# Linear attention with a highway layer on one core: batch 5's queries turned by DMA, one more x block added on GpSimd, and a new list of steps

## The chip, the core and the metric

The kernel runs on one core of a Trainium2 chip. The core has five engines with an instruction queue each: TensorE (PE: matrix products, and turning blocks by a product with the identity), VectorE (DVE), ScalarE (ACT), GpSimd (POOL), and SyncE (SP), which here only issues DMAs. Every queue runs in order: an instruction that waits holds up all that stand behind it. Sixteen DMA engines move data between HBM and the core's SBUF; TensorE writes into PSUM. The metric is the time of one execution on the device in microseconds (us); lower is better.

## The reference, cut to what matters

Eight batches, eight heads, 576 tokens, 64 channels per head; all inputs and the output are float32.

```python
# attention: q, k, v are (8, 8, 576, 64)
q_s = exp(q - max(q, -1));  q_s = q_s / sum(q_s, -1)      # softmax over channels
k_s = exp(k - max(k, 2));   k_s = k_s / sum(k_s, 2)       # softmax over tokens
kv  = einsum('bhsd,bhse->bhde', k_s, v)                   # 64 x 64 per head
x   = einsum('bhsd,bhde->bhse', q_s, kv)                  # then (4608 tokens, 512)
# highway layer: w_h, w_t are (512, 512)
H = maximum(x @ w_h, 0)
T = 1 / (1 + exp(-(x @ w_t + b_t)))
out = T * H + (1 - T) * x
```

## The kernel before

The kernel never subtracts the maxima. It works in float16 between the float32 loads and stores. The layer's output is written as x + (1 + tanh) * max(ph, -x/2), where ph comes from halved weights from which the identity was taken (`less_one`, `cast_weight` with 0.5), and tanh from half of the gate.

All 64 head rows of a batch are handled as four blocks of 128 partitions (two heads each). A token index is p * 9 + n, so a batch has nine groups n of 64 tokens. Groups 0 to 7 of two batches share one tile `xT` (a pair: batches 0 and 1 are pair 0, and so on). The ninth groups of all batches are collected in `x9` and handled at the end as two more "batches", 8 and 9, of half the width.

Per batch b the steps are:

- `load`: q, k and v by one or two DMAs each, on SP. Each of the three has three buffers; the two weight matrices borrow a buffer of q and of k.
- `exp_half` on ScalarE (two for q, two for k), `cast_v` on GpSimd or `cast_v_head` on GpSimd or ScalarE.
- `q_sums` or `q_sums_tree`, then `q_recip` on VectorE, and `q_scale_v` (VectorE, batch 0) or `q_scale_p` (GpSimd) to scale the queries.
- turning the scaled queries so that channels lie on partitions: `q_trans` (TensorE, 18 matmuls a batch in three groups, into PSUM) and `q_copy` (VectorE, one per group), or `q_turn`: a DMA transpose from SBUF to SBUF, in two pieces. Which batches use `q_turn` is in the tuple `turned`.
- `kv_half` twice on TensorE (72 small matmuls in all) and `kv_norm` on VectorE.
- `x_pair` twice on TensorE gives x; `x_copy` on ScalarE or VectorE takes it out of PSUM. For batches from 3 on the ninth group comes with it and `x9_done` copies it; before, `x_left` does.
- for each of four output blocks ob: `gate` (four matmuls with w_t) and `tanh` on ScalarE; `carry` (four matmuls with w_h) and `diff` on VectorE; `blend` on VectorE.
- the rest, "+ x", in one of two ways: `add_x` on GpSimd, for the blocks named by `added`; for the others `out_tile` adds x inside PSUM, by an extra matmul of x with the identity.
- `out_tile` turns a group of a pair back to rows of tokens: four matmuls, and one more for each block that `added` doesn't name. `out_copy` takes it to SBUF, and after each fourth group a 1 MB DMA stores it. `tile9`, `tile9_copy` and `last9` do the same for the ninth groups.

The order of all this is written out by hand, or by a program that the source doesn't contain, as one list, `order`. The kernel runs through it and issues each step as it comes, so the list fixes the order on each engine's queue, and the DMA queue of SP as well. Loads of batches 0 and 1 and of the weights stand ahead of the list, in the order q 0, k 0, v 0, bias, w_t, q 1, w_h, k 1, v 1. `warm_up` and `warm_mid` are matmuls whose result nobody reads.

Of the kernel before, what the change touches and what calls it, by code (L numbers as in the profile page):

```python
# [18 lines left out]
def kernel(  # L19
# [81 lines left out]
    def load_weight(n, w, tag, parts=1):  # L101
        t = ld.tile([P, 4, N9, 64], FP32, tag=tag, name=f"w32{n}")
        w32[n] = t.rearrange("p c n d -> p (c n d)")[:, 0:2048].rearrange(
            "p (k n) -> p k n", k=4
        )
        view = w.rearrange("(k p) n -> p k n", p=P)
        step = 4 // parts
        for k_ in range(0, 4, step):
            nc.sync.dma_start(w32[n][:, k_ : k_ + step], view[:, k_ : k_ + step])
# [13 lines left out]
    for w in "qkv":  # L123
        load(0, w, 2)
    nc.sync.dma_start(brow, moe_b_t.rearrange("(k p) -> k p", p=P))
    load_weight("t", moe_w_t, "q32")
    load(1, "q")
    load_weight("h", moe_w_h, "k32", 4)
    load(1, "k")
    load(1, "v", 2)  # L130
# [28 lines left out]
    def bank(home, name, dt=FP32):  # L159
        if home == "q2":  # L160
            return two_banks(name, dt)[:, 0]
        ps = {"ht": ps_ht, "q1": ps_1, "nat": ps_nat}[home]
        return ps.tile([P, 512 if dt is FP32 else 1024], dt, tag=home, name=name)

    def warm_mid(n):
        t = bank("q1", "warm_mid")
        for _ in range(n):
            mm(t, ident, wide, True, True)
# [112 lines left out]
    turned = (6, 7)  # L281
# [140 lines left out]
    added = lambda g: ((0, 1), (0, 1), (0, 1), (0, 1, 2, 3))[g]  # L422
# [73 lines left out]
    def last9():  # L496
# [10 lines left out]
        for f in (  # L507
            add_x, blend, carry, cast_v, cast_v_head, cast_weight, diff, exp_half, gate,
            gate_bias, kv_half, kv_norm, last9, less_one, load, out_copy, out_tile, q_copy,
            q_recip, q_scale_p, q_scale_v, q_sums, q_sums_tree, q_trans, q_turn, tanh,  # L510
            tile9, tile9_copy, warm_mid, warm_up, x9_done, x_copy, x_left, x_left_copy,
            x_pair,
        )
    }
    order = [
        ("warm_up", 24), ("exp_half", 0, "q", 1), ("warm_up", 6), ("q_sums", 0, 1),
        ("exp_half", 0, "q", 0), ("q_sums", 0, 0), ("load", 2, "q"), ("cast_v", 0, 0),
        ("q_recip", 0), ("q_scale_v", 0, 4, 9), ("warm_up", 1), ("cast_v", 0, 1),
        ("q_trans", 0, 1, "q2"), ("cast_weight", "t", 1, "P"), ("q_scale_v", 0, 0, 4),
        ("q_copy", 0, 1), ("warm_up", 4), ("exp_half", 0, "k", 1), ("q_trans", 0, 2, "nat"),  # L520
        ("q_trans", 0, 0), ("q_copy", 0, 0), ("kv_half", 0, 1), ("exp_half", 0, "k", 0),
        ("kv_half", 0, 0), ("cast_weight", "t", 3, "P"), ("kv_norm", 0),
        ("cast_weight", "t", 2, "V"), ("q_copy", 0, 2), ("x_pair", 0, 0, False),
        ("x_pair", 0, 1, False, ("ht", "ht")), ("x_copy", 0, 0, "AA"), ("less_one", 0),
        ("gate_bias",), ("x_copy", 0, 1, "AV"), ("warm_up", 2), ("exp_half", 1, "q", 0),
        ("cast_weight", "t", 0, "V"), ("q_sums_tree", 1, 0), ("exp_half", 1, "q", 1),
        ("warm_mid", 5), ("cast_weight", "h", 0, "A", 0.5), ("less_one", 2),
        ("less_one", 3), ("gate", 0, 0), ("q_sums_tree", 1, 1), ("q_recip", 1),
        ("cast_weight", "h", 3, "A", 0.5), ("cast_weight", "h", 2, "A", 0.5),
        ("less_one", 1), ("x_left", 0), ("q_scale_p", 1, 0, 4), ("gate", 0, 2, "q2"),  # L530
        ("x_left_copy", 0), ("load", 2, "v", 2), ("load", 2, "k"),
        ("cast_weight", "h", 1, "A", 0.5), ("q_scale_p", 1, 4, 8), ("warm_up", 2),
        ("tanh", 0, 0), ("tanh", 0, 2), ("cast_v_head", 1, 2, "P"), ("warm_up", 2),
        ("exp_half", 1, "k", 0), ("gate", 0, 1), ("tanh", 0, 1), ("carry", 0, 0),
        ("carry", 0, 1), ("diff", 0, 0), ("q_trans", 1, 0), ("diff", 0, 1),
        ("cast_v_head", 1, 1, "P"), ("carry", 0, 2), ("q_copy", 1, 0),
        ("cast_v_head", 1, 0, "A"), ("carry", 0, 3), ("load", 3, "k"), ("q_trans", 1, 1),
        ("diff", 0, 2), ("load", 3, "q"), ("blend", 0, 2), ("exp_half", 1, "k", 1),
        ("cast_v_head", 1, 3, "A"), ("q_copy", 1, 1), ("kv_half", 1, 0), ("kv_half", 1, 1),
        ("exp_half", 2, "q", 0), ("blend", 0, 0), ("exp_half", 2, "q", 1), ("kv_norm", 1),  # L540
        ("x_pair", 1, 0, False, ("ht", "ht")), ("blend", 0, 1), ("x_copy", 1, 0, "AV"),
        ("cast_v_head", 2, 0, "P"), ("x_pair", 1, 1, False, ("ht", "q2")),
        ("q_sums_tree", 2, 0), ("x_copy", 1, 1, "AV"), ("q_scale_p", 1, 8, 9),
        ("q_trans", 1, 2), ("gate", 0, 3, "nat"), ("cast_v_head", 2, 3, "A"),
        ("q_copy", 1, 2), ("gate", 1, 0), ("q_sums_tree", 2, 1), ("tanh", 0, 3),
        ("q_recip", 2), ("carry", 1, 0), ("diff", 0, 3), ("add_x", 0, 1),
        ("cast_v_head", 2, 1, "A"), ("load", 3, "v"), ("x_left", 1),
        ("exp_half", 2, "k", 1), ("diff", 1, 0), ("blend", 0, 3), ("carry", 1, 1),
        ("diff", 1, 1), ("tanh", 1, 0), ("q_scale_p", 2, 0, 4), ("cast_v_head", 2, 2, "P"),
        ("gate", 1, 1), ("exp_half", 2, "k", 0), ("tanh", 1, 1), ("x_left_copy", 1),  # L550
        ("gate", 1, 2), ("load", 4, "q"), ("q_trans", 2, 0, "q1"), ("kv_half", 2, 0),
        ("blend", 1, 0), ("q_copy", 2, 0), ("kv_norm", 2, 0, 1), ("blend", 1, 1),
        ("q_scale_p", 2, 4, 8), ("q_scale_p", 2, 8, 9), ("carry", 1, 2), ("add_x", 0, 0),
        ("add_x", 1, 1), ("q_trans", 2, 1, "q1"), ("diff", 1, 2), ("load", 4, "v"),
        ("tanh", 1, 2), ("q_copy", 2, 1), ("exp_half", 3, "k", 0), ("exp_half", 3, "q", 0),
        ("carry", 1, 3), ("load", 4, "k"), ("cast_v", 3, 0), ("kv_half", 2, 1),
        ("x_pair", 2, 0, False, ("nat", "q1")), ("gate", 1, 3), ("blend", 1, 2),
        ("x_copy", 2, 0, "AA"), ("kv_norm", 2, 1, 2),
        ("x_pair", 2, 1, False, ("nat", "q1")), ("exp_half", 3, "q", 1), ("q_sums", 3, 0),
        ("q_trans", 2, 2, "q2"), ("x_copy", 2, 1, "AV"), ("cast_v", 3, 1), ("load", 5, "q"),  # L560
        ("carry", 2, 0), ("q_sums", 3, 1), ("q_copy", 2, 2), ("exp_half", 3, "k", 1),
        ("gate", 2, 0), ("x_left", 2), ("diff", 2, 0), ("tanh", 1, 3), ("tanh", 2, 0),
        ("carry", 2, 1), ("exp_half", 4, "q", 0), ("q_recip", 3), ("diff", 1, 3),
        ("gate", 2, 2), ("blend", 2, 0), ("gate", 2, 1), ("blend", 1, 3), ("add_x", 1, 0),
        ("load", 6, "q"), ("x_left_copy", 2), ("out_tile", 0, 1), ("q_scale_p", 3, 0, 4),
        ("tanh", 2, 2), ("diff", 2, 1), ("tanh", 2, 1), ("blend", 2, 1),
        ("q_trans", 3, 0, "q1"), ("kv_half", 3, 0), ("q_scale_p", 3, 4, 9),
        ("kv_half", 3, 1), ("out_copy", 0, 1, "A"), ("out_tile", 0, 0), ("q_copy", 3, 0),
        ("kv_norm", 3), ("out_copy", 0, 0, "A"), ("cast_v", 4, 1), ("q_trans", 3, 1, "q1"),
        ("cast_v", 4, 0), ("q_trans", 3, 2, "q2"), ("carry", 2, 2), ("q_copy", 3, 1),  # L570
        ("q_copy", 3, 2), ("x_pair", 3, 0, True), ("q_sums", 4, 0), ("add_x", 2, 1),
        ("exp_half", 4, "q", 1), ("x_copy", 3, 0, "A"), ("out_tile", 0, 2), ("diff", 2, 2),
        ("gate", 2, 3), ("load", 5, "k"), ("out_copy", 0, 2, "A"), ("x_pair", 3, 1, True),
        ("carry", 2, 3), ("q_sums", 4, 1), ("q_recip", 4), ("load", 5, "v"),
        ("blend", 2, 2), ("x_copy", 3, 1, "A"), ("out_tile", 0, 3), ("carry", 3, 0),
        ("add_x", 2, 0), ("out_copy", 0, 3, "A"), ("x9_done", 3), ("load", 6, "v"),
        ("diff", 3, 0), ("tanh", 2, 3), ("out_tile", 0, 4), ("exp_half", 5, "q", 0),
        ("gate", 3, 0), ("q_scale_p", 4, 0, 4), ("q_scale_p", 4, 4, 9), ("gate", 3, 1),
        ("tanh", 3, 0), ("diff", 2, 3), ("blend", 3, 0), ("out_copy", 0, 4, "A"),
        ("q_trans", 4, 0, "q1"), ("carry", 3, 1), ("exp_half", 4, "k", 1),  # L580
        ("out_tile", 0, 5), ("q_copy", 4, 0), ("diff", 3, 1), ("q_trans", 4, 1, "q1"),
        ("tanh", 3, 1), ("gate", 3, 2), ("q_copy", 4, 1), ("kv_half", 4, 1),
# [105 lines left out]
```

## Time and profile before

| what | value |
|---|---|
| median of 5 runs | 129.31 us (128.53 to 129.94) |
| the profiled execution | 128.05 us |
| its span in the profile | 125.9 us |
| read from HBM, written | 30.41 MB, 9.44 MB |
| share of the DMA queue, over 16 engines' span | 85.1% |
| granted clock of TensorE, mean | 0.986 |

The profile counts from the first instruction. Rows of the timeline give a start, a length (of several instructions where "xN" stands), the engine, the line, the operation, "out<-in" by the program's names, and in brackets how long the engine had been idle before and what ended that. Tiles are named as in the program: `eq` and `ek` are the exponentials of q and k, `pq` and `qsT` the turned queries in PSUM and in SBUF, `qsD` those turned by DMA, `psk` and `kvn` the product of k and v, `px` and `xT` x, `pt` and `ph` the gate and the carry, `dd` and `g` the results of `diff` and `blend`, `nat` an output tile, `o` its copy.

The times that matter for what follows: the first gate starts at 17.80 us, the eight matmuls of `x_pair` of batch 1 at 29.95, `kv_half` of batch 3 at 52.02. Two pieces of batch 6's `q_turn` are issued from 81.88 on, of batch 7's from 92.50 on. The last matmul starts at 121.90, the last store is issued at 122.55.

### The profile page before, as it was taken

To read this page: it belongs to the slowest core of one execution; us is meant where nothing else is said; L and a number is where in the kernel's file an instruction comes from. 1 tells how busy PE (TensorE), PEld (TensorE's weight loads), DVE (VectorE), ACT (ScalarE), POOL (GpSimd) and SP (SyncE) were. 2 spreads that over 40 slices of the span, in tenths; PEclk is the share of its full clock that TensorE was granted. 3 is DMA by queue.
4 is the path that set the end of the run, shared out by engine and by line. 5 is a ranking of instruction groups with operands and counts; after the bars stand their busy time and mean duration, and the time that the engine had idled before them with its cause. 6 is when DMAs were issued, how large, how long until landed. Compare 5 with 4: busy or idle time off the path is not lost.

```text
span 125.9 us, 3361 instructions
## 1 busy us (share of the span) xinstructions
PE 111.5 (89%) x1375; PEld 62.0 (49%) x1375; DVE 96.4 (77%) x179; ACT 93.2 (74%) x130; POOL 75.6 (60%) x71
## 2 busy tenths in 40 slices
PE   4998599585599989999999998999999999999940
PEld 1344443252235534746554475555556455589820
DVE  1079749299958999899799988879966549799960
ACT  4156085995877698688998988999998895576640
POOL 2005623960779577996972895699797224855500
PEclk9999999999869999999999999999999999999999
DMA  3999999999999999999999999969427716008994
GB/s 103 386 402 404 391 403 408 411 413 410 405 411 411 407 406 412 413 402 411 420 409 409 405 412 412 424 154 278 164 50 165 303 81 260 5 42 359 421 366 150
DMA packets 20583, 41.24 MB, mean 327 GB/s; under 512 B 5460, under 2 KB 5976, under 8 KB 19544
## 3 DMA queue, kind: packets, MB, share of 16 engines
q1 hardware_dynamic: 20568, 41.03, 85.1%
q8 instruction: 10, 0.16, 0.5%
q14 instruction: 5, 0.04, 0.1%
HBM read 30.41 MB, written 9.44 MB: 316 GB/s over the span
## 4 chain that ended last, share of the span: by engine, by line
PE 51%; DMA 24%; DVE 12%; ACT 5%; issue 2%; POOL 2%; DVEq 1%; POOLq 1%; SPq 0%
PE ph L64 19%; PE pt L64 18%; DMA v<-in_v_dram 10%; DMA w32h<-in_moe_w_h_dram 10%; PE nat L64 7%; DMA q<-in_q_dram 4%; DVE g L417 3%; PE pq L69 3%; PE px L64 2%; DVE r L228 2%; DVE dd L409 2%; ACT pt L396 1%; DVE qsT L278 1%; PE psk L64 1%; DVE kvn L217 1%
## 5 line engine op out<-in xcount | busy, mean ns | idle before, releaser
L258 POOL TENSOR_TENSOR eq<-eq,r 128x1024 f16<-128x1024 f16 (+2 forms) x16 | 29.8, 1879 | 9.6 <-DVE r L246 8.7
L64 PE MATMUL ph<-xT,w16h 128*128 128x512 f16 x128 | 33.4, 387 | 2.3 <-ACT w16h L114 1.6
L64 PE MATMUL pt<-xT,w16t 128*128 128x512 f16 x128 | 32.8, 388 | 0.0
L409 DVE SCALAR_TENSOR_TENSOR dd<-xT,ph 128x512 f16<-128x512 f16 x32 | 21.5, 678 | 10.4 <-PE ph L64 9.2
L396 ACT ACTIVATE pt<-pt,bt 128x512 f32<-128x512 f32 (+1 forms) x40 | 24.5, 622 | 6.7 <-PE pt L64 6.5
L428 POOL TENSOR_TENSOR g<-g,xT 128x512 f16<-128x512 f16 x19 | 21.7, 1154 | 9.1 <-DVE g L417 8.3
L417 DVE SCALAR_TENSOR_TENSOR g<-pt,dd 128x512 f16<-128x512 f32 (+1 forms) x40 | 24.7, 627 | 2.3 <-ACT pt L396 1.1
L178 ACT ACTIVATE eq<-q 128x1152 f16<-128x1152 f32 x16 | 18.4, 1165 | 5.5 <-DMA q<-in_q_dram 5.5
L64 PEld LDWEIGHTS <-w16h 128*128 128x128 f16 x160 | 14.4, 99 | 14.7 <-issue 2.3
L64 PEld LDWEIGHTS <-w16t 128*128 128x128 f16 x160 | 14.9, 99 | 13.2 <-issue 1.9
L189 POOL CAST v<-v 128x1152 f16<-128x1152 f32 x12 | 14.3, 1209 | 11.5 <-DMA v<-in_v_dram 11.4
L178 ACT ACTIVATE ek<-k 128x1152 f16<-128x1152 f32 x16 | 18.7, 1172 | 2.1 <-DMA k<-in_k_dram 2.1
L228 DVE TENSOR_REDUCE r<-eq 128x18 f32<-128x1152 f16 x12 | 16.0, 1344 | 5.3 <-ACT eq L178 5.3
L468 ACT COPY o<-nat 128x512 f32<-128x512 f32 x28 | 16.6, 592 | 4.5 <-PE nat L64 4.0
L64 PE MATMUL nat<-ident,g 128*128 128x128 f16 x142 | 16.2, 219 | 0.1
L64 PEld LDWEIGHTS <-g 128*128 128x128 f16 x144 | 12.4, 98 | 6.5 <-DVE g L417 1.1
L64 PE MATMUL warm<-wide,ident 128*128 128x512 f16 x41 | 11.8, 444 | 1.8 <-DVE wide L149 1.8
L361 ACT CAST xT<-px 128x1024 f16<-128x1024 f32 x10 | 10.2, 1018 | 1.8 <-PE px L64 1.5
L69 PE MATMUL pq<-ident,eq 128*128 128x128 f16 x108 | 9.0, 219 | 2.4 <-POOL eq L258 1.8
L278 DVE COPY qsT<-pq 128x1024 f16<-128x1024 f16 (+1 forms) x18 | 9.9, 552 | 1.5 <-PE pq L69 1.1
L69 PEld LDWEIGHTS <-eq 128*128 128x128 f16 x108 | 6.9, 98 | 5.7 <-POOL eq L258 2.1
L64 PEld LDWEIGHTS <-ident 128*128 128x128 f16 x46 | 4.9, 109 | 8.2 <-issue 3.4
(53 smaller groups left out, 105.7 us busy)
## 6 DMA issues: line engine op xcount, KB each, us to landing
out_dram<-o SPq DMA_DIRECT2D x8, 1024.0 KB, 4.6
q<-in_q_dram SPq DMA_DIRECT2D x7, 1152.0 KB, 13.6
k<-in_k_dram SPq DMA_DIRECT2D x7, 1152.0 KB, 13.4
v<-in_v_dram SPq DMA_DIRECT2D x5, 1152.0 KB, 14.5
v<-in_v_dram SPq DMA_DIRECT2D x6, 576.0 KB, 12.1
q<-in_q_dram SPq DMA_DIRECT2D x2, 576.0 KB, 4.1
k<-in_k_dram SPq DMA_DIRECT2D x2, 576.0 KB, 6.6
w32t<-in_moe_w_t_dram SPq DMA_DIRECT2D x1, 1024.0 KB, 10.6
```

The source lines that it names most:

```text
L64: mm = lambda o, l, r, st, sp: nc.tensor.matmul(o, l, r, start=st, stop=sp, skip_group_check=True)
L69: nc.tensor.matmul(o, i, ident, is_transpose=True, start=True, stop=True, skip_group_check=True,)
L178: nc.scalar.activation(dst[b][:, :, 2 * a : 2 * a + 2, :], in32[which][b][:, 2 * a : 2 * a + 2].rearrange("p c n d -> p n c d"), AF.Exp,)
L189: nc.gpsimd.tensor_copy(o, i)
L228: nc.vector.reduce_sum(qsum[b][:, :, h], eq[b][:, :, h, :], axis=AX.X)
L258: nc.gpsimd.tensor_mul(e, e, r.broadcast_to(list(e.shape)))
L278: nc.vector.tensor_copy(qsT[b][:, :, n0:n1, :], turned_q.pop((b, g)))
L396: nc.scalar.activation(ps, ps, AF.Tanh, bias=bt2[:, ob : ob + 1], scale=0.5)
L409: nc.vector.scalar_tensor_tensor(dd, xv(ob), -0.5, ps, op0=ALU.mult, op1=ALU.max)
L417: nc.vector.scalar_tensor_tensor(gv(ob), th, 1.0, dd, op0=ALU.add, op1=ALU.mult)
L428: eng.tensor_add(gv(ob), gv(ob), xv(ob))
L468: copy(rows_of_four((g, n // 4))[:, n % 4, :], nat.pop((g, n)))
```

## The change

Four things change:

1. `turned` becomes (5, 6, 7): batch 5's queries are turned by two DMA transposes; its three `q_trans` and three `q_copy` leave the list. They are cut at group 5, not 4.
2. `added` names block 2 too for pairs 1 and 2: four more `add_x` on GpSimd (batches 2 to 5), and 16 matmuls less in `out_tile`.
3. The loads ahead of the list move into it, and the whole list is remade. Q of batch 1 is now loaded first and Q of batch 2 ahead of V and K of batch 1.
4. `warm_mid` takes a name and a bank; three calls stand in the list, one after the last step.

```diff
-    for w in "qkv":
-        load(0, w, 2)
-    nc.sync.dma_start(brow, moe_b_t.rearrange("(k p) -> k p", p=P))
-    load_weight("t", moe_w_t, "q32")
-    load(1, "q")
-    load_weight("h", moe_w_h, "k32", 4)
-    load(1, "k")
-    load(1, "v", 2)
+    def load_bias():
+        nc.sync.dma_start(brow, moe_b_t.rearrange("(k p) -> k p", p=P))
...
-    def warm_mid(n):
-        t = bank("q1", "warm_mid")
+    def warm_mid(n, i=None, home="q1"):
+        t = bank(home, "warm_mid" if i is None else f"warm_{i}")
...
-    turned = (6, 7)
+    turned = (5, 6, 7)
...
-    added = lambda g: ((0, 1), (0, 1), (0, 1), (0, 1, 2, 3))[g]
+    added = lambda g: ((0, 1), (0, 1, 2), (0, 1, 2), (0, 1, 2, 3))[g]
...
     order = [
+        ("load", 1, "q"), ("load", 0, "q", 2), ("load", 0, "k", 2), ("exp_half", 1, "q", 0),
+        ("q_sums_tree", 1, 0), ("load_bias",), ("exp_half", 0, "q", 0), ("load", 0, "v", 2),
+        ("warm_up", 24), ("warm_mid", 5), ("exp_half", 1, "q", 1), ("cast_v", 0, 0),
...
+        ("q_scale_v", 0, 4, 9), ("warm_mid", 2, 0), ("load_weight", "t", "q32"),
+        ("q_scale_p", 1, 0, 4), ("q_scale_v", 0, 0, 4), ("load_weight", "h", "k32", 4),
...
+        ("cast_weight", "h", 1, "A", 0.5), ("load", 2, "q"), ("less_one", 2),
+        ("q_trans", 0, 1, "q2"), ("warm_up", 1), ("load", 1, "v", 2), ("q_copy", 0, 0),
+        ("q_copy", 0, 1), ("x_pair", 0, 0, False), ("x_copy", 0, 0, "AA"), ("less_one", 3),
+        ("load", 1, "k"), ("gate_bias",), ("q_trans", 1, 0), ("less_one", 0),
...
+        ("load", 2, "k"), ("exp_half", 2, "q", 0), ("load", 2, "v", 2), ("q_copy", 1, 0),
+        ("warm_up", 2), ("q_scale_p", 1, 4, 8), ("x_copy", 0, 1, "AV"),
+        ("cast_weight", "t", 3, "P"), ("load", 3, "q"), ("warm_up", 2),
+        ("exp_half", 2, "q", 1), ("cast_weight", "t", 2, "V"), ("q_copy", 0, 2),
+        ("x_left", 0), ("x_left_copy", 0), ("q_sums_tree", 2, 0), ("warm_up", 2),
+        ("cast_weight", "t", 1, "P"), ("cast_weight", "h", 0, "A", 0.5), ("gate", 0, 0),
+        ("cast_weight", "h", 3, "A", 0.5), ("tanh", 0, 0), ("q_sums_tree", 2, 1),
...
+        ("x_pair", 4, 1, True), ("exp_half", 6, "q", 1), ("add_x", 2, 2), ("x9_done", 4),
+        ("q_turn", 5, 5, 9), ("x_copy", 4, 1, "A"), ("cast_v", 6, 0), ("cast_v", 5, 1),
+        ("gate", 3, 3), ("out_tile", 0, 6), ("exp_half", 5, "k", 0), ("diff", 3, 0),
+        ("blend", 3, 1), ("diff", 3, 3), ("gate", 3, 0), ("q_sums", 6, 1), ("add_x", 2, 0),
+        ("out_copy", 0, 6, "A"), ("tanh", 3, 0), ("q_turn", 5, 0, 5), ("carry", 4, 0),
+        ("carry", 4, 2), ("kv_half", 5, 1), ("diff", 4, 0), ("blend", 3, 0),
+        ("kv_half", 5, 0), ("load", 7, "v"), ("tanh", 3, 3), ("kv_norm", 5),
+        ("out_tile", 0, 7), ("add_x", 2, 1), ("exp_half", 6, "q", 0), ("gate", 4, 0),
+        ("tanh", 4, 0), ("gate", 4, 2), ("add_x", 3, 0), ("add_x", 3, 2), ("diff", 4, 2),
+        ("add_x", 3, 1), ("q_sums", 6, 0), ("x_pair", 5, 0, True), ("blend", 3, 3),
...
+        ("tanh", 9, 3), ("blend", 9, 2), ("diff", 9, 3), ("tile9", 3, 3), ("tile9", 2, 3),
+        ("tile9_copy", 2, 3, "A"), ("tile9_copy", 3, 3, "V"), ("blend", 9, 3), ("last9",),
+        ("warm_mid", 2, 3),
     ]
```

On SP's queue the loads now stand as q 1, q 0, k 0, bias, v 0, w_t, w_h, q 2, v 1, k 1, k 2, v 2, q 3, q 4, v 3, k 3, q 5, v 4, k 4, k 5, v 5, q 6, v 6, q 7, then the first output block, the two pieces of batch 5's `q_turn`, v 7, k 6, the second output block, batch 6's `q_turn`, k 7, the third output block, batch 7's `q_turn`. Before, after v 5 came the first output block, then v 6, k 6, k 7, q 7, v 7, the second output block and batch 6's `q_turn`; q 6 stood ahead of k 5.

## The prediction

> **What bounds the kernel now.** I read the page's busy shares and 40 slices, then the chain of waits, then TensorE's timeline, then the DMA rows.
>
> ```profile
> PE 111.5 (89%) x1375; PEld 62.0 (49%) x1375; DVE 96.4 (77%) x179; ACT 93.2 (74%) x130; POOL 75.6 (60%) x71
> PE   4998599585599989999999998999999999999940
> DMA  3999999999999999999999999969427716008994
> ```
>
> Two limits follow each other. The DMA digits stand at 9 up to slice 26, about 82 us: inputs arrive as fast as they can. TensorE (PE) is ragged for its first ten or so slices and solid from slice 14 to the end. So early on, the order of loads decides; later, the number of matmuls.
>
> ```profile
> 18.42 12.86 DMA v<-in_v_dram
> 31.42 0.67 POOL v L197
> 32.09 0.64 POOL eq L258
> 32.77 0.28 PE pq L69 x2
> ```
>
> The chain around 32 us (start, length): TensorE waits for batch 1's last queries, scaled by GpSimd (POOL), which stood behind a cast of batch 2's V, which waited for its load. TensorE's windows (PE busy, granted clock) show the second price:
>
> ```profile
> 31.00:32.00 1.00, 0.00 (x0) 1.00 1.05 415
> 32.00:33.00 1.00, 0.23 (x3) 1.00 1.05 408
> 34.00:35.00 1.00, 1.00 (x4) 0.50 1.03 408
> 36.00:37.00 1.00, 1.00 (x4) 0.50 1.03 406
> 38.00:39.00 1.00, 1.00 (x7) 1.00 1.05 415
> ```
>
> After the hole the clock is halved for some 3.4 us: 1.7 us of matmul time lost.
>
> ```profile
> 44.76 2.24 POOL L189 CAST v<-v 128x1152 f16<-128x1152 f32 x2 [1.12 <-DMA v<-in_v_dram]
> 64.82 2.24 POOL L189 CAST v<-v 128x1152 f16<-128x1152 f32 x2 [0.90 <-DMA v<-in_v_dram]
> 78.17 0.22 PE L64 MATMUL px_l<-qsT,kvn 64*64 64x64 f16 x2 [0.32 <-DVE kvn L217]
> ```
>
> The timeline's first two rows give landings of V of batches 3 and 5. Seven loads lie between: (64.82 - 44.76) / 7 = 2.87 us a load of 1.18 MB. The third is the start of x_pair 5, my measuring point.
>
> **A count of TensorE's work.** From starts in the timeline, a gate or carry of four 512-wide matmuls takes 0.86 us (batches 8 and 9: 0.44), a turning matmul 0.057 (0.45 for 8), kv_half 0.42, x_pair 0.34 to 0.40, an out_tile of six 0.34. Along the list this makes 92.5 us before. Time minus work ahead is the debt: kv_half 3 has 26.9 us ahead of it and starts at 52.0, debt 25.1; x_pair 5 has 51.3 and starts at 78.2, debt 26.9; the last matmul ends at about 122.1, debt 29.5.
>
> **Part 1, matmuls removed.** 18 turning matmuls of batch 5 (18 x 0.057 = 1.0 us) and, with block 2 of x no longer added in PSUM for pairs 1 and 2, 2 x 8 = 16 of 0.056 (0.9 us). Work falls to 90.6 us; it lies where TensorE is solid, so 1.9 us is the gain if debts stay. VectorE loses three q_copy (2 x 0.687 + 0.283 = 1.7 us), worth nothing by itself while TensorE is the bound.
>
> **Part 2, added on GpSimd.** Four add_x of 1.154 us (row L428), 4.6 us. What waits behind: add_x(2,2) stands before the casts that kv_half 5 needs. GpSimd takes V 5 at 61.9 (below), scales batch 5 to 67.5, then add_x 1.1 and two casts of 1.1 each: ready at 70.8. kv_half 5 has 45.0 us ahead and with a debt of 27 asks at 72. add_x(3,2) precedes scaling of batch 6, which waits for VectorE's reciprocal anyway (a 2.69 us wait in row 79.95 before); those of pair 2 come after the scaling of batch 7. I cost them at nothing, with about 1 us of cover; without it, up to 1.1 us for each of the first two.
>
> **Part 3, the DMA turns of batch 5.** Two instructions on SP. All loads before them keep the stream full, and V 5 is now one load earlier in it (q 6 follows): 64.8 - 2.9 = 61.9. q 6, v 6, q 7 land at 64.8, 67.7, 70.6, the first output block (1.05 MB) at 73.1. The turns are issued when GpSimd has scaled: the reciprocal comes at 63.3 by VectorE's queue, 2.3 + 1.9 us of scaling, so 65.6 and 67.5. Both queue behind that output. Their length:
>
> ```profile
> 92.40:95.70 3.30, 3.30 (x26) 1.88 (x25) 2.13 (x4) 3.00 (x5) 3.30 (x3) 1.00 0.41 79
> qsD<-eq SPq DMA_TRANSPOSE x4, 3.3
> ```
>
> The window (last two columns: DMA share, GB/s) holds one turn of 8 of a batch's 18 blocks: 0.41 x 3.3 = 1.35 us of all engines, so 18/8 x 1.35 = 3.0 us a batch. [...] v 7 and k 6 stand behind the turn on SP, k 7 behind that of batch 6: they land near 79, 82 and 90.5, and kv_half 6 and 7 ask near 85.5 and 95.5; hidden. The two warm matmuls put at the very end (0.43 us) lie beside the last store (issued at 122.55, 2 us to the end).
>
> **Part 4, the list.** q 1 is loaded first, so batch 0 and w_t arrive one load (2.9 us) later: V 0 ends at 15.1 instead of 12.2, w_t at 17.7 instead of 14.9. q 2 moves ahead of v 1 and k 1; V and K of batch 1 are complete at 29.9 instead of 27.0. K and V of batch 2 end at 36.1 as before. The first gate ran at 17.8; now its x copy stands on ScalarE behind exp of q 2 (lands 24.2), so it runs near 25.7. w_h arrives at 21.3 either way and its last cast follows at 27.9, so carries start there. Then kv_half 1 waits for exp of k 1 (29.9, two exps and a cast: 32.7), x_pair 1 ends at 35.2, kv_half 2 waits for V 2 (36.1) and two GpSimd casts: 37.5. carry(1,1) ends at 39.3 with 14.4 us of work behind it: debt 24.9, against 23.7 before at 40.2. Between the warm-up's end near 11.8 us (31 matmuls end at 10.9 before, 35 now) and kv_half 0 near 14.9 TensorE idles 3 us, and is thin after; add 0.7 us for a halved clock: debt 25.6, 1.9 behind.
>
> [...] I take 0.7 and leave 0 to 1.7 for the range.
>
> From 40 to 48 us VectorE runs without pause in both lists (sums of batch 3 sit between the diffs); kv_half 3 comes at 24.0 + 26.8 = 50.8, debt 26.8, 1.7 behind. Up to x_pair 5 before lost 1.8 us more; I give the new list 1.5 (fewer copies): it has 47.9 us ahead, 47.9 + 28.3 = 76.2, just as the turn lands.
>
> **Sum.** From x_pair 5: 90.6 - 47.9 = 42.7 us of work, plus the 2.6 us before lost from there to its end, minus 0.3, as VectorE has less left when gate(9,0) runs (5.6 against 8.5 us of durations). 76.2 + 42.7 + 2.3 = 121.2 against 122.1: -0.9. The span becomes 125.0, the profiled run's 128.05 becomes 127.15. It lies 1.26 below the median of 129.31 (runs 128.53 to 129.94), so 128.4.
>
> **Rivals.**
> *Forecast, 0.42:* as summed, own range 127.2 to 129.6. Half of it is over 1% faster or nearly so: I give 0.2 to faster, 0.22 to within.
> *Everything saved is kept, 0.20:* the early debt is made up where VectorE has fewer copies, and turns land at 74.6; end 74.9 + 42.7 + 1.9 = 119.5, 126.7 us. For: TensorE need not be solid before 50 us. Against: VectorE has no pause there.
> *The turn of batch 5 lands late, 0.24; slower:* every middle load takes 12 to 14 us from issue to landing ("q<-in_q_dram" 13.6). If the stream is still that deep at 67.5, the second half lands at 67.5 + 13 = 80.5, 4.3 late: 132.7; half as deep, 131. TensorE runs in order, so all behind x_pair 5 moves with it. It decides from x_pair 5 after 78.4 on (0.9 + 1.3 past 76.2). For: GpSimd scales batch 5 only behind a cast that waits for V 5. Against: SP must first wait for the output block's copy near 62, which drains the stream.
> *Four full engines, 0.14:* from 50 to 76 us VectorE, ScalarE and GpSimd each have about 23 us of work for TensorE's 24 (rows' durations summed along the list, less what successive ones overlap: 0.60 us apart where the row says 0.68), GpSimd some 2 us more than before. 1.5 us more of waits: 129.9.
>
> **Numbers.** About 1% is what a measurement of this kernel can tell from no change. Faster: 0.2 + 0.2 = 0.40. Within: 0.22 + 0.06 of the full engines = 0.28. Slower: 0.24 + 0.08 = 0.32. The range 126.2 to 131.6 leaves out the ends of second and third case.
>
> **What would show it.** TensorE near 90 us without warm-ups; first gate at 25 to 26 us; kv_half 3 at 50 to 52; x_pair 5 at 76 waiting for qsD at most 1 us; no hole from 80 to the tail. A first gate before 22 or an x_pair 5 after 78.4 proves me wrong, as does a GpSimd add as the releaser of output tiles.

## The result, and the profile after

The changed kernel took 127.76 us in the median of 44 runs, the kernel before 129.17 us in 79. The ratio is 0.9949, 95% interval [0.9924, 0.9974]: a small gain. It is not the quotient of the two medians (0.989), because it compares only the fast runs of each kernel, those within 1.5% of its fastest. The prediction was 128.4 us. Run once more beside the last experiments, the same changed kernel came to 0.9865 [0.9816, 0.9914]. The two intervals do not meet, so ratios from different groups of runs can't be compared more finely than about 1%. Below, small differences are therefore read in the traces, from one event to another.

The profiled execution took 128.16 us, its span is 126.2. That of before had 128.05 and 125.9. Taken alone the two would say "no change"; why they mislead comes out of the clock row, in 9 below. From the page of the changed kernel, the busy shares and three rows of the 40 slices:

```profile
PE 111.1 (88%) x1345; PEld 61.7 (49%) x1345; DVE 95.7 (76%) x176; ACT 92.0 (73%) x130; POOL 79.5 (63%) x75
PE   4997314899998999999999999999997999999960
PEclk9999965569999999999999999999999999999999
DMA  3999999999999999999999999989997530089994
```

Before, TensorE was ragged to slice 13; now the digits are thin in slices 4 to 6 (12 to 22 us) and nearly solid behind that, with one 7 near 97 us. The clock row has a half-speed stretch where TensorE is thin. From the timeline (TensorE) and the DMA rows of the changed kernel, the two that answer to x_pair 5 and to the turns:

```profile
76.83 0.22 PE L64 MATMUL px_l<-qsD,kvn 64*64 64x64 f16 x2
```

```profile
qsD<-eq SPq DMA_TRANSPOSE x6, 5.3
```

x_pair 5 starts at 76.83 us with no wait in brackets: batch 5's turned queries were there. Its two pieces were issued at 67.92 and 69.78 and landed at 73.64 and 74.75.

The head, in windows of 6 us (stretch, its length, busy time of PE, PEld, DVE, ACT and POOL with the number of instructions, granted clock, DMA share, GB/s):

```profile
12.00:18.00 6.00, 1.49 (x74) 0.94 (x73) 5.15 (x9) 1.77 (x2) 3.00 (x3) 0.91 1.05 410
18.00:24.00 6.00, 2.86 (x21) 1.99 (x21) 4.59 (x7) 0.63 (x1) 6.00 (x7) 0.50 1.05 407
24.00:30.00 6.00, 6.00 (x44) 3.00 (x41) 3.80 (x11) 5.34 (x8) 1.42 (x3) 0.74 1.04 411
```

TensorE works 1.49 of the first 6 us while VectorE works 5.15. In the next window the clock is 0.50: it was halved from 16.9 to 27.2 us. The first gate starts at 29.01 us; 25.7 was predicted. TensorE's two long waits of that stretch:

```profile
14.60 0.48 PE L64 MATMUL psk<-v,ek 64*64 64x65 f16 x36 [2.68 <-POOL v L185]
20.79 1.89 PE L69 MATMUL pq<-ident,eq 128*128 128x128 f16 x16 [4.28 <-DVE eq L250]
```

The second is for VectorE's scaled queries. VectorE's and GpSimd's rows show what came before them:

```profile
14.89 1.25 DVE L236 TENSOR_TENSOR t<-t 128x288 f16<-128x288 f16 x1
17.96 1.88 DVE L248 CAST r<-r 128x32 f16<-128x32 f32 x1
```

```profile
14.83 1.15 POOL L185 CAST v<-v 128x1152 f16<-128x1152 f32 x1 [0.28 <-DMA v<-in_v_dram]
17.30 2.50 POOL L254 TENSOR_TENSOR eq<-eq,r 128x1024 f16<-128x1024 f16 x1 [1.32 <-DVE r L248]
```

Two small instructions of VectorE end just behind an instruction of GpSimd that they lie over: 16.14 behind 15.98, and 19.84 behind 19.80. The scaling on GpSimd took 2.50 us; the eight others of its size (the next one at 21.75) took 1.90.

A hole that before did not have, from ScalarE's and TensorE's timelines:

```profile
94.46 2.22 ACT L174 ACTIVATE ek<-k 128x1152 f16<-128x1152 f32 x2 [2.10 <-DMA k<-in_k_dram]
```

```profile
97.20 0.33 PE L64 MATMUL nat<-ident,g 128*128 128x128 f16 x3 [0.73 <-ACT o L464]
```

ScalarE waits 2.10 us for K of batch 7. The copy of an output tile stands behind it on ScalarE, and TensorE needs the bank which that copy frees: 0.73 us lost. K 7 was issued at 85.97 and landed at 94.38.

### The profile page after: what moved, and what is told of

Same layout as the page of the kernel before. It is cut to its first block, busy times and chain, and to the rows that moved or that the text cites. A ratio compares the mean times of both kernels' runs of the same rounds, so it can differ in the third digit from the quotient of the medians.

```text
span 126.2 us, 3307 instructions
## 1 busy us (share of the span) xinstructions
PE 111.1 (88%) x1345; PEld 61.7 (49%) x1345; DVE 95.7 (76%) x176; ACT 92.0 (73%) x130; POOL 79.5 (63%) x75
## 4 chain that ended last, share of the span: by engine, by line
PE 69%; DVE 11%; DMA 6%; ACT 4%; POOL 3%; issue 2%; SPq 1%; DVEq 1%; ACTq 0%
PE pt L64 23%; PE ph L64 21%; PE nat L64 8%; DMA k<-in_k_dram 6%; PE pq L69 5%; PE psk L64 4%; PE px L64 4%; PE warm L64 3%; POOL eq L254 2%; ACT ek L174 2%; DVE dd L405 2%; DVE r L248 1%; DVE eq L250 1%; PE px_l L64 1%; SPq L94 1%
## 5 line engine op out<-in xcount | busy, mean ns | idle before, releaser
L254 POOL TENSOR_TENSOR eq<-eq,r 128x1024 f16<-128x1024 f16 (+2 forms) x16 | 30.3, 1911 | 13.3 <-ACT pt L392 7.1
L64 PE MATMUL ph<-xT,w16h 128*128 128x512 f16 x128 | 31.7, 379 | 0.0
L424 POOL TENSOR_TENSOR g<-g,xT 128x512 f16<-128x512 f16 x23 | 25.9, 1156 | 7.5 <-DVE g L413 6.7
L185 POOL CAST v<-v 128x1152 f16<-128x1152 f32 x12 | 13.6, 1148 | 14.7 <-DMA v<-in_v_dram 14.7
L64 PEld LDWEIGHTS <-w16h 128*128 128x128 f16 x160 | 14.6, 98 | 13.0 <-issue 1.1
L64 PEld LDWEIGHTS <-w16t 128*128 128x128 f16 x160 | 14.3, 98 | 11.1 <-issue 0.5
L64 PE MATMUL warm<-wide,ident 128*128 128x512 f16 x45 | 14.1, 464 | 1.8 <-DVE wide L144 1.8
L64 PE MATMUL nat<-ident,g 128*128 128x128 f16 x142 | 14.6, 219 | 0.7 <-ACT o L464 0.7
L64 PEld LDWEIGHTS <-g 128*128 128x128 f16 x144 | 11.4, 98 | 6.5 <-issue 1.6
L64 PE MATMUL psk<-v,ek 64*64 64x65 f16 x576 | 6.8, 194 | 3.5 <-POOL v L185 3.1
L64 PEld LDWEIGHTS <-ident 128*128 128x128 f16 x50 | 5.5, 114 | 8.7 <-issue 4.4
## 6 DMA issues: line engine op xcount, KB each, us to landing
v<-in_v_dram SPq DMA_DIRECT2D x5, 1152.0 KB, 14.6
```

Of the source, the lines that this page charges most:

```text
L64: mm = lambda o, l, r, st, sp: nc.tensor.matmul(o, l, r, start=st, stop=sp, skip_group_check=True)
L185: nc.gpsimd.tensor_copy(o, i)
L254: nc.gpsimd.tensor_mul(e, e, r.broadcast_to(list(e.shape)))
L424: eng.tensor_add(gv(ob), gv(ob), xv(ob))
```

## The experiments

Each was run beside the kernel before, and the ratios are to that. "Gate to end" is the time from the start of the first gate to the start of the last output matmul: 92.98 us in the profile above. It leaves out what the head lost. Where an expectation speaks of the "last matmul", it means the last of all, in the changed list a warming one some 0.3 us later.

**1. Is the head's loss the clock? More warming matmuls.**

```diff
-("warm_up", 6), ("q_sums", 0, 1)
+("warm_up", 16), ("q_sums", 0, 1)
...
-("kv_half", 0, 1), ("kv_norm", 0)
+("kv_half", 0, 1), ("warm_up", 18), ("kv_norm", 0)
```

> The changed list with 10 more warm-up matmuls before batch 0's kv products and 18 after them, so that TensorE doesn't stand idle between 12 and 21 us. Theory (the halved clock from 16.9 to 27.2 us delays batch 0's turned queries and x, and so the first gate at 29.0 us): the granted clock stays at full from 6.7 us on, the 16 turning matmuls take 0.9 us instead of 1.9, the first gate comes at 27 to 28 us, and the time falls by 0.8 to 1.8 us. Rival (the first gate waits for loads and casts, ScalarE's exp of q 2 above all): the clock is full, the first gate stays within 0.5 us of 29.0, and the time within 0.5 us of the changed kernel's.

Measured: 0.9875 [0.9821, 0.9929]. The clock stays full to 39.0 us, the first gate starts at 26.94. But in the profiled execution the end came no earlier: the last output matmul starts at 122.16 (121.99 without the warming). TensorE's timeline:

```profile
20.77 1.17 PE L69 MATMUL pq<-ident,eq 128*128 128x128 f16 x16 [0.29 <-DVE eq L250]
39.36 0.43 PE L64 MATMUL psk<-v,ek 64*64 64x65 f16 x15 [1.41 <-issue]
```

The sixteen turning matmuls take 1.17 us instead of 1.89, and start at the same time as without (20.79): the clock accounts for 2.07 us of the first gate, the wait for VectorE is untouched. The second row shows a new hole of 1.41 us in the middle of a kv_half, with no releaser that the profile knows, and from 39.0 us on, shortly before its end, the clock was halved for 3.41 us. What that hole is comes out in 10 and 11. The loss behind it isn't in every execution: the profiled one took 128.18 us at a mean clock of 0.978, the other four runs behind the ratio 126.4 to 127.1 us at 0.993 or more.

**2. Would an earlier K 7 close the hole at 97 us?** Load 7 k moved up behind load 6 k.

```diff
-("load", 6, "k"),
+("load", 6, "k"), ("load", 7, "k"),
...
-("load", 7, "k"), ("kv_half", 6, 1),
+("kv_half", 6, 1),
```

> The changed list with the load of batch 7's K issued right behind that of batch 6, ahead of the second output block and of batch 6's turns. Theory (K 7 landed at 94.4 because it stood behind batch 6's turns and then shared the DMA engines with batch 7's; ScalarE waited 2.1 us for it with an output copy behind, TensorE 0.73): K 7 lands before 90, no idle time of TensorE near 97 us, time 0.7 us less. Rival (another wait ends just behind it, batch 6's turns now late behind K 7): x_pair of batch 6 moves from 88.7 to 90 or later and the time is the same or longer.

Measured: 1.0269 [1.0197, 1.0341]. From the list of TensorE's waits (total, times, longest) and its windows, columns as above:

```profile
PE px L64 <- DMA qsD<-eq: 2.1, 1, 2.1
```

```profile
90.00:96.00 6.00, 3.88 (x37) 2.01 (x33) 2.37 (x4) 3.86 (x6) 6.00 (x6) 1.00 1.06 279
```

The load goes ahead of batch 6's two turns, which land at 89.81 and 92.18 us instead of 86.54 and 87.79; x_pair 6's second half starts at 92.22, and TensorE stands for 2.12 us. Gate to end is 94.42, 1.4 more. So K 7 behind that turn cost 0.7 us, and K 7 ahead of it 2.1.

**3. What was the turn of batch 5 worth?** `turned` back to (6, 7), with three q_trans and three q_copy put into the new list.

```diff
-turned = (5, 6, 7)
+turned = (6, 7)
...
-("q_turn", 5, 5, 9),
+("q_trans", 5, 1, "q1"),
...
-("q_turn", 5, 0, 5), ("carry", 4, 0), ("carry", 4, 2), ("kv_half", 5, 1),
+("carry", 4, 0), ("q_trans", 5, 0, "q1"), ("carry", 4, 2), ("q_copy", 5, 0), ("kv_half", 5, 1),
```

> The changed list with batch 5 turned by TensorE again (18 matmuls, three VectorE copies) where the DMA turns stood; all else as changed. Theory (TensorE is the bound from 29 us on, so each removed matmul counts): 1.0 us longer. First rival (the DMA turns cost more than they save, by the loads that wait behind them): the same or shorter. Second rival (the copies are what counted, VectorE having no pause there): 2 us longer or more.

Measured: 1.0052 [1.0009, 1.0096]; gate to end 94.74, 1.76 more than with the turn. One window and one row of TensorE:

```profile
66.00:72.00 6.00, 5.40 (x57) 3.02 (x54) 3.93 (x9) 5.30 (x8) 6.00 (x5) 1.00 1.03 414
```

```profile
69.72 0.61 PE L69 MATMUL pq<-ident,eq 128*128 128x128 f16 x8 [0.53 <-DVE x L309]
```

1.0 us is the matmuls, 0.53 a wait behind VectorE. The latter is partly of my making, since I chose where the six steps stand. What is left, 0.2 us or more, wasn't traced.

**4. What were the additions on GpSimd worth?** Third-block x of pairs 1 and 2 back in PSUM, the four add_x left out of the list.

```diff
-added = lambda g: ((0, 1), (0, 1, 2), (0, 1, 2), (0, 1, 2, 3))[g]
+added = lambda g: ((0, 1), (0, 1), (0, 1), (0, 1, 2, 3))[g]
```

> The changed list with block 2 of x added in PSUM again for pairs 1 and 2 (16 matmuls more, four GpSimd additions less). Theory (TensorE bound): 0.9 us longer, nothing gained on GpSimd. Rival (GpSimd, busy 79.5 us and without a pause from 66 to 78 us, holds something up): no longer than the changed kernel, or shorter.

Measured: 0.9977 [0.9927, 1.0027], which can't be told from the change. Gate to end is 93.02: the same, with 0.9 us more work. TensorE is busy for 6.00 of 6.00 us from 96 to 102, where the changed kernel has 5.26. That can't be put down to the extra matmuls: in this execution the clock was halved for 13.65 us and the first gate came at 30.39, while K 7 landed at 94.35 as before, and ScalarE, being later, didn't wait for it. So the two profiles differ by more than the additions, and this test leaves their worth open. 12 takes it up.

**5. The hole by itself: the exponentials of K 7 put behind the output copy.**

```diff
-("x_copy", 6, 1, "A"), ("exp_half", 7, "k", 0), ("gate", 6, 2), ("add_x", 4, 0), ("exp_half", 7, "k", 1),
+("x_copy", 6, 1, "A"), ("gate", 6, 2), ("add_x", 4, 0),
...
-("tanh", 6, 2), ("tanh", 6, 0),
+("tanh", 6, 2), ("exp_half", 7, "k", 0), ("exp_half", 7, "k", 1), ("tanh", 6, 0),
```

> The changed list with the two exps of batch 7's K moved on ScalarE behind the second-last output copy of pair 1 and tanh(6,2), so that no output copy stands behind the late load. Theory (the 0.73 us hole of TensorE at 97 us is that copy waiting behind exps that wait for K 7; the saved x matmuls were lost in it): no hole over 0.3 us from 90 to 102 us, first gate to last matmul 92.6 us instead of 93.25, time 0.7 us less than the changed kernel. Rival (kv_half 7 then waits for the exps by as much): the hole moves to kv_half 7 and nothing is gained.

Measured, on three runs: 0.9896 [0.9811, 0.9982]; gate to end 92.09, 0.9 less. The first gate (29.04) stands where it did. The window where the hole was:

```profile
96.00:102.00 6.00, 6.00 (x124) 3.62 (x123) 3.88 (x8) 4.36 (x7) 3.37 (x4) 1.00 0.71 238
```

The hole is gone, but K 7 landed at 92.26 here, 2.1 us earlier than in the first profile, so this execution doesn't show that the moved exponentials closed it. 10, with the same move and K 7 at 94.28, has 6.00 of 6.00 us there too; 1, without the move, with K 7 at 94.56 and TensorE 0.8 us later at x_pair 6, has 5.92.

**6. VectorE and GpSimd in the head.** Batch 1's second tree sum and its reciprocal go behind the scaling of batch 0's queries, with 16 and 6 warming matmuls to keep the clock.

```diff
-("q_sums_tree", 1, 1), ("q_recip", 0), ("kv_half", 0, 0), ("q_recip", 1),
+("q_recip", 0), ("kv_half", 0, 0),
...
-("q_scale_p", 1, 0, 4), ("q_scale_v", 0, 0, 4),
+("q_scale_v", 0, 0, 4), ("q_sums_tree", 1, 1), ("q_recip", 1), ("q_scale_p", 1, 0, 4),
```

> The changed list with the warm-up as in the run with the warm head (6 instead of 18 in the second gap) and with batch 1's second sum and reciprocal moved on VectorE behind the scaling of batch 0. Theory (VectorE's sum and scaling of batch 0 and 1 lie beside GpSimd's casts and scaling there and hold each other up: a 0.39 us addition took 1.25, a 0.18 us copy 1.88): scaling of batch 0 ends at 17.5 to 18.5 us instead of 20.7, the copy takes under 0.5 us, first gate at 25 to 26 us (26.9 with the warm head alone), time 0.5 to 1 us less than with the warm head alone. Rival (the first gate is set by ScalarE's exps of q 2, that land at 22.7 to 24.4 us): scaling ends early, first gate stays at 26.5 or later, no gain.

Measured: 0.992 [0.9886, 0.9955]. The clock is full from 6.2 us to the end, the first gate starts at 25.84: 1.1 us earlier than with warming alone. On VectorE the scaled queries are done at 17.4 us instead of 20.7, and two rows of the same sum, with GpSimd idle beside them, are short:

```profile
17.33 0.45 DVE L235 TENSOR_TENSOR t<-eq 128x576 f16<-128x576 f16 x1
17.81 0.31 DVE L236 TENSOR_TENSOR t<-t 128x288 f16<-128x288 f16 x1
```

The small cast of batch 0's reciprocals was not freed: it took 1.13 us where under 0.5 was expected, and ended at 16.69, just behind a cast on GpSimd (14.85 to 16.65) that took 1.80 instead of 1.15. So the gain is more that of the order than of the hold-ups.

The last output matmul starts at 120.61, and gate to end is 94.78: 3.2 us were won at the first gate, 1.4 are left at the end. TensorE is busy for 5.68, 4.62 and 5.49 us in the windows from 30, 36 and 84 us, where the changed kernel has 5.95, 5.64 and 6.00: 1.8 us of new waits, less the K 7 hole, which isn't there. Of the waits in these windows 1.01 us is the hole of 1 again, at 37.3 us; 0.69 are two waits for casts of V on GpSimd and 0.35 one for an output copy, work that TensorE now reached before its inputs.

**7. The parts without the list.** Before's list with the turn of batch 5 in place of q_trans and q_copy, and the four add_x beside those that stood there.

```diff
-turned = (6, 7)
+turned = (5, 6, 7)
...
-("q_scale_p", 5, 4, 9), ("out_tile", 0, 7),
+("q_scale_p", 5, 4, 9), ("q_turn", 5, 0, 4), ("q_turn", 5, 4, 9), ("out_tile", 0, 7),
```

> The kernel before with the two parts of the change and its old list: the DMA turns of batch 5 behind its scaling, the four additions behind the others of their batch. Theory (a turn that is issued while the stream is full lands late, and TensorE waits in order): the turns are issued near 74 us behind v 7, which lands at 81.5; they land at 84.5, x_pair of batch 5 moves from 78.2 to about 84.5, and the time is 3 to 5 us longer than before. Rival (the loads ahead hardly matter, and the matmuls removed count): 1 to 2 us shorter than before.

Measured: 1.095 [1.0876, 1.1024], the slowest of all. From the waits and the windows of TensorE:

```profile
PE px_l L64 <- DMA qsD<-eq: 5.1, 1, 5.1
PE nat L64 <- POOL g L428: 3.6, 3, 2.5
```

```profile
84.00:90.00 6.00, 4.71 (x28) 2.00 (x28) 0.69 (x1) 3.09 (x5) 4.68 (x4) 0.52 0.99 210
```

The turns, issued at 73.60 and 78.32, land at 82.67 and 85.25. x_pair 5 starts at 85.28 and the clock is halved from 84.2 to 91.0. In this list output tiles wait for GpSimd's additions, for 3.6 us in all. The two parts that save 1.9 us of matmuls cost 9.5% where the loads around them and GpSimd's queue were not rearranged with them. That is 12 us where 3 to 5 were expected: the turn's wait was forecast well, the waits for GpSimd and the 6.83 us of half clock were not.

**8. Before, with its hole at 31 us filled** by eight warming matmuls.

```diff
-("q_trans", 1, 2), ("gate", 0, 3, "nat"),
+("warm_mid", 8), ("q_trans", 1, 2), ("gate", 0, 3, "nat"),
```

> The kernel before with 8 warm-up matmuls in its hole at 31 to 32.8 us. Theory (the halved clock after the hole costs 1.7 us): the granted clock stays full from 6 us on, and the time falls by 1 to 1.7 us, more than the whole change brought. Rival (the matmuls slowed there would have waited anyway, or the clock falls elsewhere): within 0.5 us of before.

Measured: 1.0052 [1.0021, 1.0084]: nothing won. The clock was halved at 16.3 to 19.7 us instead, and the rest was full. The last output matmul starts 1.35 us earlier than before. SP's timelines, of this kernel and of before, show the last store:

```profile
121.20 0.37 SPq L502 DMA_DIRECT2D out_dram<-o  x1
```

```profile
122.55 0.37 SPq L502 DMA_DIRECT2D out_dram<-o  x1
```

It is issued 1.35 us earlier and lands at 124.47, against 124.48: 2.9 us from the end of its issue, against 1.6. In this execution what TensorE won was lost in the last stores; one profile can't say how often.

**9 to 12. The changed kernel again, and combinations,** run side by side. 10 joins 1 and 5; 11 joins 5 and 6; 12 joins 4 and 5.

> The changed kernel once more, beside the three below on one chip. Theory: the ratio to the kernel before is again between 0.990 and 1.000, the first gate of batch 0 starts near 29 us where the clock is halved early and near 27 where it is not, first gate to last matmul 93.2 us as in its first profile. Rival (the gain seen was a matter of the clock's chance alone): 1.000 or more, and the stretch from first gate to last matmul differs by over 1 us from 93.2.

> The changed kernel with more warming matmuls in the head and with the exponentials of K7 behind the output copy of batch 6. Theory: the head's 2.0 us of later first gate and the 0.7 us hole at 96 to 97 us are separate losses, so the two gains add: first gate near 27, no hole at 96 to 102, 1.0 to 1.5 us below the changed kernel beside it. Rival: an earlier head is given back by later holes (K and V loads, the turned pieces of batch 6), so it is no more than 0.7 us below, which the exponentials alone bring.

> The changed kernel with batch 1's second key sum behind the scaling of batch 0's turned queries, 16 and 6 warming matmuls, and with the exponentials of K7 behind the output copy of batch 6. Theory: the first gate near 25.8, last matmul near 120.0 to 120.5, 1.0 to 1.7 us below the changed kernel beside it. Rival: batch 6's turned pieces bound the second steps of x_pair 6 at 88 to 90 us, and the earlier start goes into that wait: within 0.7 us of the changed kernel.

> The changed kernel with the exponentials of K7 behind the output copy of batch 6, and the third-block x additions of pairs 1 and 2 back on TensorE (16 matmuls of 0.056 us, 0.9 us, no additions on GpSimd). Theory: with the K7 hole gone nothing hides these matmuls: first gate to last matmul near 93.2 us, 0.9 us more than the 92.35 of the kernel with the exponentials moved alone. Rival: the additions never were on the path, first gate to last matmul 92.4 and the time the same.

| | ratio | first gate | last output matmul | gate to end |
|---|---|---|---|---|
| 9 changed, again | 0.9865 [0.9816, 0.9914] | 27.71 | 120.60 | 92.90 |
| 10 | 0.9968 [0.9915, 1.002] | 26.76 | 121.93 | 95.17 |
| 11 | 0.9859 [0.9806, 0.9912] | 25.62 | 119.72 | 94.10 |
| 12 | 1.0005 [0.9946, 1.0065] | 27.72 | 121.08 | 93.36 |

9 is the same program as the profile after; this execution took 126.80 us where the first took 128.16. Its clock row on the page:

```profile
PEclk9999975699999999999999999999999999999997
```

Half clock lasts 6.83 us here (17.3 to 24.1), 10.24 there. The first gate is 1.30 us earlier, kv_half 3 1.3, x_pair 5 1.25, the last output matmul 1.39: one further stretch of 3.41 us at half clock cost 1.3 us at the first gate, and nothing behind gave it back. That is why the first profile, against one of before with a single such stretch, shows no gain. Seven profiles have this same head (the changed kernel's two, 2, 3, 4, 5 and 12), and in all of them the first gate follows the end of the half clock: ends at 24.1, 24.2, 25.0, 27.2, 27.2, 29.5 and 29.9 us go with first gates at 27.7, 27.7, 28.0, 29.0, 29.0, 30.0 and 30.4. So where the stretches lie counts as much as their number: 3 had as many as the first profile, but they began 2.2 us earlier.

In 10 and 11 the hole of 1 came back. TensorE's timelines, 10 and then 11:

```profile
39.38 0.43 PE L64 MATMUL psk<-v,ek 64*64 64x65 f16 x15 [1.61 <-issue]
```

```profile
38.12 0.22 PE L64 MATMUL psk<-v,ek 64*64 64x65 f16 x3 [0.79 <-issue]
```

Counted through the trace, the matmul that starts late is number 351 in all four kernels with more warming (1, 6, 10, 11). 1 and 10 have 28 warming matmuls more than the change, 6 and 11 have 16, and in the first two the hole lies 12 matmuls earlier in the kv_half accordingly. It goes with a position in TensorE's program, not with data. The page counts ten packets of 16 KB on a queue named "instruction", and in each of the four one of them starts just ahead: at 37.18, 36.13, 36.95 and 35.96 us; matmul 351 follows 2.2 to 2.4 us later. In 9 the packet starts at 38.02 and matmul 351 at 40.40, without a pause before it. That the packets bring TensorE's program I take from the name of their queue and from their fit with matmul 351; no run shows it directly. In all four, and in 9, the packet starts 0.4 to 0.9 us before this kv_half. In 9 matmul 351 lies behind the kv_half, among long carry matmuls, 2.4 us later. The warming matmuls put ahead of it move it into the kv_half's short ones: TensorE is ready for it 0.8 to 1.4 us after the packet's start, and waits. What starts these packets, and whether the full DMA engines (a share of 1.04 to 1.05 from 36 to 42 us) make them later, was not tried.

So the forecast that the gains of 10 add fell: in its profile 0.95 us were won at the first gate, then 1.61 lost in the hole and more in the 3.41 us of half clock that followed. (As in 1, five of the eight runs behind its ratio kept a mean clock of 0.993 or more, and took 127.1 to 127.7 us instead of the profile's 128.25.) In 11 the end is 0.88 us earlier than in 9, but by the runs the two are the same. No version beat the changed kernel by more than the runs can tell.

12 has the head of 9 to 0.01 us up to kv_half 5, so the two can be laid side by side. The end is 0.48 us later: 0.9 of matmuls more, less a wait of this kind that 9 has and 12 has not (TensorE's timeline of 9):

```profile
87.87 0.33 PE L64 MATMUL nat<-ident,g 128*128 128x128 f16 x3 [0.35 <-ACT o L464]
```

Against 5, which has the exponentials moved and the additions on GpSimd, gate to end is 1.27 longer. With the K 7 hole gone, the 0.9 us counts, as the theory had it. The ratio of 12 against 9, 1.4% higher, is more than the trace bears out; the two profiles' spans differ by 0.7 us. Three of the eight runs behind 12's ratio had a mean clock of 0.935 to 0.946, below all of 9's (0.953 to 0.966), which may be the rest.

9 also shows that the K 7 hole isn't in every execution: there K 7 landed at 93.0 and TensorE has 6.00 of 6.00 us at 96 to 102. So the hole is a loss that comes and goes, and closing it is worth less per run than the 0.73 us of one profile. How K 7 comes late in some executions shows in the 16 reports that the trace has of this load, of which the last makes the landing. In the first profile 15 reports of K 7 came by 92.16 us and the last at 94.38, 2.0 us behind the start of a 16 KB instruction packet (92.36). 1, 3, 10 and 12 have the same: the packet starts at 91.9 to 93.1 us and the last report follows 2.0 to 2.1 us behind it, 1.4 to 2.0 us after the fifteenth. In 4 the packet came only at 93.9, and the last report was 0.8 us behind the fifteenth. In 5, 6, 9 and 11, where that packet starts at 91.7 or before, the 16 reports lie within 1.3 us. So this hole, too, seems to come with an instruction packet. How a packet would hold up one report of a load is not shown, and no experiment moved the packet.

## Why the prediction was right, step by step

The sum had three debts (time minus work ahead of that point). Here they stand beside both profiles of the changed kernel; work ahead of the three points is 24.0, 47.9 and 90.6 us. (Before's last debt is the forecast's; 122.1 - 92.5 is 29.6.)

| point: time, debt | before | predicted | first profile | second profile |
|---|---|---|---|---|
| kv_half 3 starts | 52.0, 25.1 | 50.8, 26.8 | 52.1, 28.1 | 50.8, 26.8 |
| x_pair 5 starts | 78.2, 26.9 | 76.2, 28.3 | 76.8, 28.9 | 75.6, 27.7 |
| last output matmul ends | 122.1, 29.5 | 121.2, 30.6 | 122.2, 31.6 | 120.8, 30.2 |

- **Part 1, the 1.9 us of matmuls: right.** Taking the turn back costs 1.76 us of gate to end (1.0 in matmuls), taking the additions back 0.46 (12 against 9) or 1.27 (12 against 5), for 0.9 in matmuls. As predicted, the head's later start eats into the gain: the debt at the end rose by 0.7 us in the second profile, 1.1 in the forecast, and 2.1 in the first profile, which is all of the gain.
- **Part 2, additions at nothing: right in this list.** No wait of TensorE names a GpSimd addition. The cover was real: in the old list (7) output tiles waited 3.6 us for them.
- **Part 3, the turn's landing: late by 1.5 us in the forecast.** The output block was put at 73.1 and landed at 72.58; the turn was put at 76.2, 3.1 us behind it, and its second piece landed 2.2 behind it (74.75). No run shows where the 74.6 comes from, at which the rival "everything saved is kept" has the turns land; the first profile has 74.75. My row held one piece alone; here the first piece was through 1.1 us before the second. The rival "lands late" did not come about: SP had issued nothing but the output block since 58 us, so that only this and q 7 were still ahead of the turn, as the argument against the rival had it. It is no phantom, though: 2 and 7 have exactly this wait, 2.1 and 5.1 us long.
- **Part 3, "K 7 lands at 90.5, hidden": wrong.** It landed at 94.38 and 93.0. I had added up the stream at 2.87 us a load. In the first profile its packets run from 87.2 us, as batch 6's turns end, to 92.4, the third output block's from 91.0 on; in the second from 87.3 to 92.6. Why they took 5 us isn't shown. The rest of the first profile's delay is the one late report told of under 9. It cost 0.73 us in one profile, nothing in the other.
- **Part 4, the head: the term mis-sized was the clock.** The first gate was predicted near 25.7. With the clock full and batch 0 scaled first it starts at 25.84 and 25.62 (6, 11). The changed kernel has 29.01: of the 3.2 us, 1.1 come from VectorE's order, with its hold-ups by GpSimd (1 against 6), 2.1 from the halved clock (after against 1). I had put 0.7 on the clock in all, range to 1.7; the second profile lost 0.8 to 1.0. Here the clock fell at 16.9 us, after gaps of 2.68 us (11.9 to 14.6) and 0.41, and 0.4 us into the wait of 4.28; in 1 it fell during a hole of 1.41 us, before behind one of 1.82 (30.96 to 32.77). The halving behind before's 1.82 us was there to be read ahead of the forecast, and I weighed it too lightly in the head. The runs give no threshold: in 11 a hole of 0.79 us, in 6 one of 1.01, did not halve the clock.
- **Between kv_half 3 and x_pair 5: 0.8 to 0.9 us lost where 1.5 was taken.** The rival "four full engines" fell with it. TensorE is busy nearly without a break there (24.69 of 24.73 us in the first profile), with no q_copy of batch 5 to wait for.
- **The profile against the median.** I put the median 1.26 us above the profiled execution, as before's was. For the changed kernel it lies 0.4 below. The executions differ by whole stretches of half clock: of the 44 runs, the nine with a mean clock of 0.964 or more took 126.5 to 127.5 us, the seventeen at 0.941 or less 128.15 to 129.7. So this gap is chance, and an offset taken from one profile is worth no more than a stretch. That 128.4 came so near 127.76 is luck in part: the profiled execution was forecast 1.0 us too short (127.15 against 128.16), the step from there to the median 1.7 us too long.

## What to carry to other kernels

Price a DMA that replaces matmuls by what stands around it in the DMA queue: the same turn of batch 5 was free behind a rearranged queue and cost 5.1 us of waiting in the old one. Before two profiles are compared, count the stretches at half clock in each; one here cost 1.3 us at the first gate, about as much as the whole change brought (1.4 between the medians). And when one hole is closed or a head is made earlier, ask what arrives too late next: here it was other data, and once, as I read it, the instructions themselves.

## What the runs showed of the hardware

- Half-clock stretches inside the kernel lasted 3.41, 6.83, 10.24 or 13.65 us, whole multiples of 3.41, and their number differed between two executions of one program. While TensorE worked 2.86 of 6 us (window 18 to 24 above) the clock stayed at half.
- Some instructions of VectorE and GpSimd took longer where they lay over each other: a sum of 0.31 us took 1.25, a small cast took 1.13 to 1.88 us where one of a quarter more elements took 0.12 to 0.18, and a scaling on GpSimd of 1.90 us took 2.50. Not all did: the eight scalings of 1.90 us also had instructions of VectorE beside them.
- TensorE stood 0.8 to 1.6 us at one fixed position in its program, 2.2 to 2.4 us behind the start of a 16 KB instruction packet. That it waited for its own instructions is my reading of that; no run shows it directly.
- In five profiles a load's last report came 2.0 to 2.1 us behind the start of such a packet, and up to 2.2 us after its other fifteen.
